# Output tiles, a weight's place in the queue and the casts of a fused attention and soft-MoE kernel

## The chip, the cores and the metric

The kernel runs on one core of a Trainium2 chip. The metric is the device time of one execution in microseconds, as the median of several runs. Smaller is better.

## The reference

Attention with two kinds of masks (four heads see a sliding window of 32 keys, four heads a dilated one), followed by a soft mixture of experts on its output:

```python
scores = scale * np.matmul(q, k.transpose(0, 1, 3, 2))      # B=8, H=8, S=576, D=64
scores = np.where(masks[None, :, :, :], scores, -1000000000.0)
attn = softmax(scores)                                       # over the keys
x = np.matmul(attn, v)  ->  [4608, 512]                      # all tokens, heads side by side

logits = x @ phi                                             # [4608, 32]: 8 experts x 4 slots
slot_input = softmax(logits, axis=0).T @ x                   # [32, 512]
for e in range(E):                                           # E = 8
    h = np.maximum(slot_input[e] @ w1[e], 0.0)               # w1: [8, 512, 1024]
    slot_out[e] = h @ w2[e]                                  # w2: [8, 1024, 512]
out = softmax(logits, axis=1) @ slot_out                     # [4608, 512] float32
```

`softmax` stands for the reference's steps of maximum, exponential and division. The output has 4608 x 512 x 4 bytes, 9.44 MB.

## The kernel before

Attention runs in 32 units (8 batches, 4 pairs of heads each). The raw batch data and, later, the weights live in eight buffers of SBUF, `home0` to `home7`, each 128 partitions by 8192 halves (16 KB a partition). `home{b}` first holds q, k and v of batch `b`. When that batch is done, it takes the weights of expert `e = b`: w1 in the first 4096 columns and w2 in the other 4096. All these loads convert float32 to float16 on their way and are issued by POOL, in the order in which they stand in the program.

`load_w1(e)` (L239) is one transfer of 1 MB written. `load_w2(e)` (L255) depends on the expert, counted from 0:

- experts 0 to 5: one transfer of 1 MB (L262);
- expert 6: by columns; `load_half(6, 0)` (L250) brings the first 256 columns, and the other half is loaded later, in between the pieces of expert 7;
- expert 7: by columns too, and each half of the columns in two pieces (`PIECES`, L271), with the second half of expert 6 ahead of its own second half.

In the loop over units, at `u % 4 == 2`, expert `u // 4` has its w1 loaded (experts 0 to 6) and its w2 (experts 0 to 5). After the loop come w1 of expert 7, then w2 of experts 6 and 7.

From `tail.__enter__()` on (L698) PE, DVE and ACT run in the order that the program has by hand. The experts go in four pairs: `expert_in(pr)` multiplies the slots by w1 of the two experts of a pair (L752) and applies the relu on ACT (L760); `expert_turn(pr)` transposes the result (L766) and copies it to `hTp` on DVE (L771); `expert_out(e, side)` multiplies by w2 and adds up in the PSUM tile `sop` (L781). The pairs are interleaved:

```python
for pr in range(4):
    expert_turn(pr)
    if pr < 2:
        expert_in(pr + 2)
    if pr == 1:
        front_rows(B - 1)
    if pr < 3:
        expert_out(2 * pr)
        expert_out(2 * pr + 1)
```

So the fourth pair's `expert_in`, which needs w1 of experts 6 and 7, stands ahead of `expert_out` of experts 2 to 5.

The last pair's `expert_out` and the output go by `SIDES`: first columns 0 to 255 of `sop`, then 256 to 511. On each side, the sums of experts 6 and 7 are added, the side of `sop` is cast to `so` (its first half on ACT at L840, its second half on DVE at L841), and the first six of twelve output tiles are made for this side. The remaining six tiles follow with all 512 columns at once.

`finish_tile(i, d0, d1)` (L810) makes one output tile: for each of its 2 or 4 blocks of 128 rows, one product on PE (L822) into one of six rotating PSUM tiles, and an eviction with the row's scale, in turn on ACT (L826) and DVE (L828), into the tile `ot`. SP then sends it. Tile 0 of the first side is sent block by block (L832), every other one whole (L834). There are four `ot` tiles in `home0` to `home3`, which the weights of experts 0 to 3 have left by then; tile `i` uses `ots[i % 4]`, so it can be written when tile `i - 4` has been sent. Within an `ot`, the two sides lie in separate halves.

Of the kernel before, what the change touches and what calls it, by code (L numbers as in the profile page):

```python
# [9 lines left out]
FP32 = mybir.dt.float32  # L10
# [15 lines left out]
DMODEL = H * D  # L26
E_EXP = 8
# [33 lines left out]
def kernel(  # L61
# [10 lines left out]
    nc = tc.nc  # L72
# [6 lines left out]
    big = ctx.enter_context(tc.tile_pool(name="big", bufs=1))  # L79
# [5 lines left out]
    for n, (nm, ten, by) in enumerate((("qp", q, nc.sync), ("kp", k, nc.scalar))):  # L85
        first[nm] = stage[0:NP, 768 * n : 768 * n + 768].rearrange("p (g x) -> p g x", g=2)
        by.dma_start(
            out=first[nm],
            in_=ten[0, 0:2].rearrange("h s d -> (h s) d").rearrange("(g p r) d -> p g (r d)", g=2, r=RP),
# [106 lines left out]
    def spread_v(b):  # L196
        nc.vector.tensor_copy(
            out=vd[b % 2][:, :, 0:D], in_=raws[b]["vd"].rearrange("p h r d -> p (h r) d")
        )
# [39 lines left out]
    def load_w1(e):  # L239
        t = homes[e]  # L240
        w1t = t[:, 0:4096].rearrange("p (c f) -> p c f", c=4)
        nc.gpsimd.dma_start(  # L242
            out=w1t.rearrange("p c f -> p (c f)"),
            in_=moe_w1[e].rearrange("(p c) f -> p (c f)", p=128),
        )
        w_tiles[e] = [w1t, t[:, 4096:8192].rearrange("p (c f) -> p c f", c=8)]

    def load_half(e, side):
        d0, d1 = SIDES[side]
        nc.gpsimd.dma_start(  # L250
            out=w_tiles[e][1][:, 0:8, d0:d1],
            in_=moe_w2[e].rearrange("(p c) f -> p c f", p=128)[:, 0:8, d0:d1],
        )

    def load_w2(e):  # L255
        w2t = w_tiles[e][1]
        w2_from = moe_w2[e].rearrange("(p c) f -> p c f", p=128)
        if e == E_EXP - 2:
            load_half(e, 0)
            return  # L260
        if e < E_EXP - 2:
            nc.gpsimd.dma_start(  # L262
                out=w2t.rearrange("p c f -> p (c f)"), in_=w2_from.rearrange("p c f -> p (c f)")
            )
            return
        w2t = w_tiles[e][1] = w2t.rearrange("p c f -> p (c f)").rearrange("p (s c f) -> p s c f", s=2, c=8)
        for n, (d0, d1) in enumerate(SIDES):
            if n == 1:
                load_half(e - 1, 1)
            for c0, c1 in PIECES:  # L270
                nc.gpsimd.dma_start(out=w2t[:, n, c0:c1], in_=w2_from[:, c0:c1, d0:d1])  # L271
# [46 lines left out]
    def scores(u):  # L318
        b, hp = unit(u)
        qT, kT = qTs[u], kTs[u]  # L320
        tiles = []
        for part in range(2):
            st = ps_s.tile([128, 2, 512], FP32, name=f"s{u}_{part}", tag="s")
            if hp < 2:
                todo = [(160 * i, 128 * i, 128 * i, QW) for i in range(3)] if part == 0 else [
                    (0, 384, 384, QW), (QW, 512, 512, 64)]
            else:
                todo = [(DW * cc, CL * (2 * cc + part), CL * (2 * cc + part), CL) for cc in range(2)]
                todo += [(DW * cc + CL, None, CL * (2 * cc + part) + 128, 16) for cc in range(2)]
            for at, k0, q0, n in todo:  # L330
                for g in range(2):
                    ks = q0 - 32 * g - 64 * (at // DW) if k0 is None else k0
                    nc.tensor.matmul(  # L333
                        st[:, g, at : at + n],
                        kT[64 * g : 64 * g + 64, ks : ks + 128],
                        qT[64 * g : 64 * g + 64, q0 : q0 + n],
                        start=True,
                        stop=True,
                    )
            tiles.append(st)  # L340
        return tiles

    def softmax_parts(u, tiles):
        b, hp = unit(u)
        for part in range(2):
            st = tiles[part]
            if hp < 2:
                n = (480, 224)[part]
                pr = raw_pool.tile([128, 2, n], FP16, name=f"pr{u}_{part}", tag=f"pr{part}")
                nc.scalar.activation(out=pr, in_=st[:, :, 0:n], func=AF.Exp, scale=SCALE)  # L350
                for b0, nb, w in ((0, 3, QW),) if part == 0 else ((3, 1, QW), (4, 1, 64)):
                    at = (b0 - 3 * part) * QW
                    nc.vector.tensor_tensor(  # L353
                        out=Pp[:, :, b0 : b0 + nb, 0:w],
                        in0=pr[:, :, at : at + nb * w].rearrange("p h (t c) -> p h t c", c=w),
                        in1=mask[:, None, None, 0:w].broadcast_to([128, 2, nb, w]),
                        op=ALU.mult,
                    )
                continue
            if part == 0:  # L360
                pr = dil_pool.tile([128, 2, 2, 2, DW], FP16, name=f"pd{u}", tag="pd")
            nc.scalar.activation(  # L362
                out=pr[:, part].rearrange("p c e t -> p e c t"),
                in_=st[:, :, 0 : 2 * DW].rearrange("p e (c t) -> p e c t", c=2),
                func=AF.Exp,
                scale=SCALE,
            )
        if hp >= 2:
            dilated_masks(pr)
# [17 lines left out]
    def values(u):  # L387
        for half in range(2):
            normalise(u, half, value_products(u, half))
# [271 lines left out]
    for u in range(NU - 2):  # L661
        st = scores(u + 1)
        values(u)
        softmax_parts(u + 1, st)
        if u + 3 < NU:
            transposes(u + 3)
        b, ph = divmod(u - 4, 4)
        if b >= 0:
            if ph == 1:
                front_logits(b)  # L670
            elif ph == 2:
                front_rows(b)
            elif ph == 3:
                front_slots(b)
        if u == 1:
            spread_phi()
        if u >= 1:
            x_transposes(u - 1)
        if u == NU - 3:
            sixes = batch_sums()  # L680
        if u % 4 == 3 and u // 4 + 1 < B:
            spread_v(u // 4 + 1)
            select_v(u // 4 + 1)
        if u % 4 == 2 and u // 4 < E_EXP - 1:
            load_w1(u // 4)
            if u // 4 < E_EXP - 2:
                load_w2(u // 4)
        if u < 4:
            nc.vector.memset(hTp[u], 0.0)

    load_w1(E_EXP - 1)
    load_w2(E_EXP - 2)
    load_w2(E_EXP - 1)

# [32 lines left out]
        out=siT,  # L727
# [15 lines left out]
    sop = ps_so.tile([128, DMODEL], FP32, name="sop", tag="sop")  # L743
# [50 lines left out]
    for pr in range(4):  # L794
# [7 lines left out]
            expert_out(2 * pr + 1)  # L802

    so = keep.tile([128, DMODEL], FP16, name="so", tag="so")
    ots = [
        big.tile([128, 4, DMODEL], FP32, name=f"ot{i}", tag=f"home{i}") for i in range(4)
    ]
    turn = [0]

    def finish_tile(i, d0, d1):  # L810
        t0, nj = OUT_TILES[i]
        ot = ots[i % 4]
        if d1 - d0 < DMODEL:
            ot = ot.rearrange("p j d -> p (j d)").rearrange("p (s j d) -> p s j d", s=2, j=4)[:, d0 // (d1 - d0)]
        rows_out = out[t0 : t0 + 128 * nj, :].rearrange("(m j) d -> m j d", j=nj)
        for j in range(nj):
            c0, scale = t0 + j, rrow[:, OUT_COLS[i] + j : OUT_COLS[i] + j + 1]
            by_act = turn[0] % 2 == 0
            pool, tag = ((ring, "ring"), (ps_h, "h"), (ps_t, "tp"))[turn[0] % 3]
            fp = pool.tile([128, DMODEL], FP32, name=f"f{turn[0]}", tag=tag)[:, 0 : d1 - d0]  # L820
            turn[0] += 1
            nc.tensor.matmul(  # L822
                fp, ET[:, c0 : c0 + 127 * nj + 1 : nj], so[:, d0:d1], start=True, stop=True
            )
            if by_act:
                nc.scalar.activation(out=ot[:, j], in_=fp, func=AF.Copy, scale=scale)  # L826
            else:
                nc.vector.tensor_scalar(  # L828
                    out=ot[:, j], in0=fp, scalar1=scale, scalar2=None, op0=ALU.mult
                )  # L830
            if i == 0 and d0 == 0:
                nc.sync.dma_start(out=rows_out[:, j, d0:d1], in_=ot[:, j])  # L832
        if i > 0 or d0 > 0:
            nc.sync.dma_start(out=rows_out[:, :, d0:d1], in_=ot[:, 0:nj])  # L834

    for n, (d0, d1) in enumerate(SIDES):
        expert_out(E_EXP - 2, n)
        expert_out(E_EXP - 1, n)
        mid = (d0 + d1) // 2
        nc.scalar.copy(out=so[:, d0:mid], in_=sop[:, d0:mid])  # L840
        nc.vector.tensor_copy(out=so[:, mid:d1], in_=sop[:, mid:d1])  # L841
        for i in range(FIRST_TILES):
            finish_tile(i, d0, d1)
    for i in range(FIRST_TILES, len(OUT_TILES)):
# [35 lines left out]
```

## Time and profile before

| what | us |
|---|---|
| median of three runs | 184.31 (183.91 to 184.97) |
| the profiled execution itself | 184.91 |
| its span, first to last instruction | 183.1 |
| mean granted TensorE clock | 0.945 |

Busy time over the span, from the page: PE 145.5 us (79%), DVE 118.1 (64%), ACT 117.2 (64%), POOL 50.6 (28%). The queue of POOL's transfers takes 96.7% of the 16 DMA engines' span (30.68 MB), and the queue of SP's, which sends the output, 14.1% (9.82 MB). These shares are averages over stages: up to about 130 us attention keeps PE, DVE and ACT busy while the loads stream beside it; after 156 us the output stage has little work on the engines.

How to read it: the chain of waits goes back from the last instruction, at each step to what released it. The view of stretches gives, for each stretch of time, the busy time of PE, PE's weight loads, DVE, ACT and POOL with the number of instructions, and then the granted clock, the share of the DMA engines (it can pass 1, as packets overlap) and the GB/s that they moved, counted as written.

### The profile page before, as it was taken

Reading aid. Unit: us, or ns where it says so; the run is one execution under the profiler, and the core shown is the slowest. Engines: PE = TensorE matmul, PEld = TensorE weight load, DVE = VectorE, ACT = ScalarE, POOL = GpSimd, SP = SyncE. Lnnn points to the kernel's source line nnn. Section 1 sums busy time; section 2 is a strip of 40 time slices with the busy share of each in tenths; the row PEclk is TensorE's granted clock in tenths of the full one; section 3 lists DMA queues with packets and bytes.
Section 4 is the critical chain, followed back from the end, with each engine's and each line's share of the span. In section 5 each row is a group of like instructions: output and inputs, shape, how many; then the busy total and the mean of one; then the engine's idle time right before and its main releaser. Section 6 shows DMA issues by size and latency. Waiting matters only on the chain.

```text
span 183.1 us, 6162 instructions
## 1 busy us (share of the span) xinstructions
PE 145.5 (79%) x2625; PEld 101.2 (55%) x2625; DVE 118.1 (64%) x370; ACT 117.2 (64%) x218; POOL 50.6 (28%) x81
## 2 busy tenths in 40 slices
PE   0797889789889899989979988989799497559300
PEld 0665767576766676767667676667683133334000
DVE  6716896978778778787797877869610002659510
ACT  2076988885987797798799599788213111649410
POOL 7855545555554535300111010034110000000000
PEclk9999999999999999999999999999988958999955
DMA  5999999999999999999999999999999999699996
GB/s 152 192 199 204 200 204 203 201 201 206 198 204 203 200 201 205 224 213 218 217 213 220 211 218 211 224 209 220 211 222 207 195 197 124 233 380 335 430 429 259
DMA packets 31051, 41.18 MB, mean 225 GB/s; under 512 B 1712, under 2 KB 28464, under 8 KB 28720
## 3 DMA queue, kind: packets, MB, share of 16 engines
q0 software_dynamic: 25296, 30.68, 96.7%
q1 hardware_dynamic: 5520, 9.82, 14.1%
q8 instruction: 20, 0.33, 0.6%
q10 hardware_dynamic: 208, 0.29, 0.5%
q14 instruction: 7, 0.06, 0.1%
HBM read 62.02 MB, written 9.44 MB: 390 GB/s over the span
## 4 chain that ended last, share of the span: by engine, by line
DMA 49%; PE 18%; issue 14%; DVE 7%; ACT 6%; POOL 2%; POOLq 0%; ACTq 0%; DVEq 0%
DMA home<-in_moe_w_dram 29%; DMA home<-in_k_dram 9%; DMA out_dram<-ot 6%; DMA home<-in_v_dram 5%; PE sop L781 3%; PE f L822 2%; ACT pd L362 2%; PE sel L208 2%; PE l L470 2%; ACT ot L826 2%; DVE kTd L313 1%; DVE P L373 1%; DVE x L438 1%; PE rgx L452 1%; PE o L417 1%
## 5 line engine op out<-in xcount | busy, mean ns | idle before, releaser
L438 DVE TENSOR_TENSOR x<-o,rc 128x384 f16<-128x384 f32 x64 | 30.1, 483 | 0.6
L350 ACT ACTIVATE pr<-s 128x960 f16<-128x960 f32 (+1 forms) x32 | 24.9, 785 | 0.4 <-PE s L333 0.4
L362 ACT ACTIVATE pd<-s 128x640 f16<-128x640 f32 x32 | 20.9, 706 | 0.7 <-PE s L333 0.7
L167 POOL DMA_DIRECT2D home<-in_v_dram x24 | 16.5, 688 | 16.6 <-DMA home<-in_k_dram 8.7
L828 DVE TENSOR_SCALAR ot<-f,rrow 128x256 f32<-128x256 f32 (+1 forms) x26 | 13.5, 580 | 6.8 <-DMA out_dram<-ot 5.9
L826 ACT ACTIVATE ot<-f,rrow 128x256 f32<-128x256 f32 (+1 forms) x26 | 12.5, 563 | 8.3 <-DMA out_dram<-ot 6.9
L208 PE MATMUL sel<-home,pick 32*128 32x256 f16 x128 | 16.8, 291 | 0.5 <-ACT pr L350 0.5
L452 PE MATMUL rgx<-fixed,x 128*128 128x128 f16 x160 | 14.2, 220 | 3.8 <-ACT qT L313 3.5
L298 ACT COPY qT<-rgq 128x576 f16<-128x576 f16 x16 | 10.3, 641 | 10.4 <-PE rgq L293 10.4
L353 DVE TENSOR_TENSOR Pp<-pr,fixed 128x960 f16<-128x960 f16 (+2 forms) x48 | 16.4, 393 | 0.0
L428 DVE RECIPROCAL rc<-o 128x6 f32<-128x6 f32 x64 | 9.9, 174 | 9.8 <-PE o L417 9.5
L822 PE MATMUL f<-so,ET 128*128 128x256 f16 (+1 forms) x52 | 11.2, 311 | 5.0 <-ACT ot L826 2.9
L242 POOL DMA_DIRECT2D home<-in_moe_w_dram x8 | 4.2, 531 | 36.2 <-PE rgk L308 14.3
L293 PEld LDWEIGHTS <-home 96*64 96x64 f16 x384 | 11.2, 116 | 5.2 <-issue 3.1
L216 ACT CAST vp<-sel 128x512 f16<-128x512 f32 x16 | 9.4, 589 | 7.1 <-PE sel L208 6.8
L452 PEld LDWEIGHTS <-x 128*128 128x128 f16 x160 | 9.6, 97 | 7.2 <-issue 5.1
L458 ACT COPY xT<-rgx 128x512 f16<-128x512 f16 x16 | 9.7, 607 | 4.5 <-PE rgx L452 4.5
L313 DVE COPY kTd<-rgk 128x576 f16<-128x576 f16 x16 | 11.9, 746 | 0.4 <-PE rgk L308 0.4
L417 PE MATMUL o<-vp,Pp 128*128 128x65 f16 x288 | 12.0, 197 | 0.0
L189 POOL DMA_DIRECT2D home<-in_k_dram x15 | 9.8, 650 | 7.7 <-DMA home<-in_q_dram 6.8
L470 PE MATMUL l<-xT,phi 128*128 128x288 f16 x64 | 10.1, 295 | 1.9 <-ACT qT L298 1.7
L313 ACT COPY qT<-rgq 128x576 f16<-128x576 f16 x16 | 10.4, 648 | 1.5 <-PE rgq L308 0.6
(114 smaller groups left out, 290.4 us busy)
## 6 DMA issues: line engine op xcount, KB each, us to landing
home<-in_moe_w_dram POOLq DMA_DIRECT2D x14, 1024.0 KB, 32.8
home<-in_q_dram POOLq DMA_DIRECT2D x15, 288.0 KB, 9.8
home<-in_k_dram POOLq DMA_DIRECT2D x15, 288.0 KB, 10.0
home<-in_v_dram POOLq DMA_DIRECT2D x16, 256.0 KB, 9.8
out_dram<-ot SPq DMA_DIRECT2D x4, 1024.0 KB, 6.7
out_dram<-ot SPq DMA_DIRECT2D x6, 512.0 KB, 3.6
out_dram<-ot SPq DMA_DIRECT2D x7, 256.0 KB, 2.7
home<-in_moe_w_dram POOLq DMA_DIRECT2D x2, 512.0 KB, 26.6
```

What stands on the lines that cost most here:

```text
L167: nc.gpsimd.dma_start(out=dst, in_=v[b, h0 : h0 + n_h, r0 : r0 + 4 * n_p, :].rearrange("h (p r) d -> p h (r d)", r=4),)
L208: nc.tensor.matmul(sel[:, n, 0], pick[rows, r].rearrange("p i j -> p (i j)"), raw[rows, :, r, :], start=(r == 0), stop=(r == 3), tile_posi ...
L313: (nc.scalar.copy if nm == "q" else nc.vector.tensor_copy)(out=dst[:, 0:S].rearrange("c (g p a) -> c g p a", g=4, a=3), in_=rg.rearrange(" ...
L350: nc.scalar.activation(out=pr, in_=st[:, :, 0:n], func=AF.Exp, scale=SCALE)
L353: nc.vector.tensor_tensor(out=Pp[:, :, b0 : b0 + nb, 0:w], in0=pr[:, :, at : at + nb * w].rearrange("p h (t c) -> p h t c", c=w), in1=mask ...
L362: nc.scalar.activation(out=pr[:, part].rearrange("p c e t -> p e c t"), in_=st[:, :, 0 : 2 * DW].rearrange("p e (c t) -> p e c t", c=2), f ...
L417: nc.tensor.matmul(to, lhs, rhs, start=(n == 0), stop=(n == len(mms) - 1), skip_group_check=True)
L438: nc.vector.tensor_tensor(out=x[:, t0 : t0 + nb, D * hl : D * hl + 2 * D].rearrange("p t (h d) -> p t h d", h=2), in0=ot[:, 0:nb, :, 0:D], ...
L452: nc.tensor.transpose(rg[:, 128 * blk : 128 * blk + 128], x[:, blk, hl : hl + 128], ident)
L470: nc.tensor.matmul(lp, phi4[:, kc].rearrange("p a s -> p (a s)"), xT[:, kc, 288 * c : 288 * c + 288], start=(kc == 0), stop=(kc == 3), ski ...
L822: nc.tensor.matmul(fp, ET[:, c0 : c0 + 127 * nj + 1 : nj], so[:, d0:d1], start=True, stop=True)
L826: nc.scalar.activation(out=ot[:, j], in_=fp, func=AF.Copy, scale=scale)
```

## The change

- There are eight `ot` tiles instead of four, two in each of `home0` to `home3`. Tile `i` uses `ots[i % 8]`.
- Tile 0 of the first side is sent whole, in one transfer, as the others are.
- w2 of expert 5 is no longer loaded in the loop but after it, behind w1 of expert 7. That puts w1 of experts 6 and 7 ahead of it in POOL's order.
- `so` is cast by one engine on each side: ACT on the first, DVE on the second.

w2 of experts 6 and 7 is loaded by columns as before.

```diff
         if u % 4 == 2 and u // 4 < E_EXP - 1:
             load_w1(u // 4)
-            if u // 4 < E_EXP - 2:
+            if u // 4 < E_EXP - 3:
                 load_w2(u // 4)
...
     load_w1(E_EXP - 1)
+    load_w2(E_EXP - 3)
     load_w2(E_EXP - 2)
     load_w2(E_EXP - 1)
...
-    ots = [
-        big.tile([128, 4, DMODEL], FP32, name=f"ot{i}", tag=f"home{i}") for i in range(4)
+    pairs = [
+        big.tile([128, 2, 4, DMODEL], FP32, name=f"ot{i}", tag=f"home{i}") for i in range(4)
     ]
+    ots = [pairs[i // 2][:, i % 2] for i in range(8)]
...
-        ot = ots[i % 4]
+        ot = ots[i % 8]
...
-            if i == 0 and d0 == 0:
-                nc.sync.dma_start(out=rows_out[:, j, d0:d1], in_=ot[:, j])
-        if i > 0 or d0 > 0:
-            nc.sync.dma_start(out=rows_out[:, :, d0:d1], in_=ot[:, 0:nj])
+        nc.sync.dma_start(out=rows_out[:, :, d0:d1], in_=ot[:, 0:nj])
...
-        mid = (d0 + d1) // 2
-        nc.scalar.copy(out=so[:, d0:mid], in_=sop[:, d0:mid])
-        nc.vector.tensor_copy(out=so[:, mid:d1], in_=sop[:, mid:d1])
+        (nc.scalar.copy if n == 0 else nc.vector.tensor_copy)(out=so[:, d0:d1], in_=sop[:, d0:d1])
```

## The prediction

> **What bounds the kernel now.** I read the chain of waits first, then the waits, the transfers of the weights, and last the output stage in stretches. The chain of waits, start and length in us:
>
> ```profile
> 121.84 24.28 DMA home<-in_moe_w_dram
> 146.12 0.04 issue
> 146.16 1.89 PE h L752 x14
> ...
> 153.55 0.65 PE sop L781 x16
> 154.20 0.02 issue
> 154.22 0.28 ACT so L840
> 154.50 0.02 issue
> 154.52 0.30 DVE so L841
> ...
> 161.48 2.68 DMA out_dram<-ot
> ```
>
> PE gets its last work from w1 of expert 7 (counted from 0), landing at 146.1. From there PE computes without a pause to the first cast of `so` at 154.22; the casts run one after the other. The rest of the chain alternates with output transfers. The waits from 140 us on say why:
>
> ```profile
> ACT ot L826 <- DMA out_dram<-ot: 6.9, 5, 1.9
> DVE ot L828 <- DMA out_dram<-ot: 5.9, 5, 1.7
> ...
> PE h L752 <- DMA home<-in_moe_w_dram: 2.6, 1, 2.6
> ```
>
> Evictions wait for a buffer whose transfer is still out: 6.9 and 5.9 us. That matters only where the DMA engines then run dry, so I cut the end into stretches (engine busy times, then granted clock, DMA share, GB/s):
>
> ```profile
> 142.40:145.80 3.40, 1.16 (x18) 0.36 (x7) 0.26 (x2) 0.32 (x1) 0.00 (x0) 1.00 1.27 196
> 145.80:152.60 6.80, 6.17 (x62) 2.20 (x61) 0.49 (x3) 0.60 (x1) 0.00 (x0) 0.50 1.44 196
> 154.30:155.50 1.20, 0.64 (x6) 0.58 (x6) 0.51 (x2) 0.52 (x2) 0.00 (x0) 1.00 0.55 75
> 155.50:156.50 1.00, 0.98 (x7) 0.52 (x6) 1.00 (x4) 1.00 (x4) 0.00 (x0) 1.00 0.17 22
> 156.50:158.00 1.50, 0.76 (x4) 0.38 (x4) 0.44 (x2) 0.51 (x2) 0.00 (x0) 1.00 0.58 203
> 160.00:160.50 0.50, 0.00 (x0) 0.00 (x0) 0.33 (x2) 0.14 (x1) 0.00 (x0) 1.00 0.45 162
> 160.50:165.50 5.00, 3.10 (x18) 1.92 (x18) 2.90 (x8) 2.82 (x8) 0.00 (x0) 1.00 1.09 384
> 165.50:166.50 1.00, 1.00 (x7) 0.51 (x5) 1.00 (x4) 1.00 (x3) 0.00 (x0) 1.00 0.38 129
> 169.00:181.40 12.40, 1.76 (x6) 0.39 (x4) 3.69 (x6) 2.95 (x5) 0.00 (x0) 0.67 1.02 427
> ```
>
> Output bytes flow from 156.5 to 181.4. Fed, the stream moves 384 GB/s while half tiles go out and 427 GB/s afterwards. The 9.44 MB are 4.19 MB of half tiles (12 tile halves) and 5.24 MB of whole tiles: 4.19/0.384 + 5.24/0.427 = 10.9 + 12.3 = **23.2 us**. The stage takes 24.9, so it starves for 1.7 us: at 156.5 to 158 (203 of 384 GB/s, 0.7 us lost), 160 to 160.5 (0.3), 165.5 to 166.5 (0.7). The output stage is bandwidth with three holes.
>
> The weights end in a long tail. At 196 GB/s all engines work; 75 GB/s at 154.3 to 155.5 is some 6 of 16, 22 GB/s after that one or two. Those laggards finish at 156.7, which is when the last piece of w2 of expert 7 lands (issued 136.63, 20.1 to landing).
>
> **The weights' order.** All weights go through one queue, landing about every 4.9 us: w1 of 5 at 131.3 (issue 92.15 + 39.1), w2 of 5 at 136.3, w1 of 6 at 141.3, w1 of 7 at 146.1, the first column half of w2 of 6 at 148.8, the two first-side pieces of w2 of 7 at 150.75 and 151.5, then 154.1, 156.1 and 156.7. Putting w2 of 5 behind w1 of 7 moves w1 of 6 to 136.3 and w1 of 7 to 141.2, and w2 of 5 to 146.1. One issue of 0.53 us on POOL moves from 96.84 to 122.4 and pushes the three issues behind it by 0.53. That costs nothing as long as the queue is full: at 121.84 it still holds w2 of 4, w1 of 5 and w1 of 6, some 15 us. Without that cover it would cost the 0.53. The last three issues on POOL wait for the landing of the transfer eight places earlier (127.31 after 127.1, 131.81 after 131.3, 136.63 after 136.3); the places are the same after the change, and a landing sits at each of those times, so they stay. SP has nothing queued then.
>
> **PE up to the first cast.** PE reaches the fourth pair's w1 products at 143.15 and no longer waits there. By rows at full clock: 16 products 1.09 (the row at 140.92), row sums 0.45, `sop` of experts 2 and 3 1.04, transposes 0.41, `hTp` 0.26, `sop` of 4 and 5 1.04, to 147.4; expert 5's half starts at 146.9, 0.8 after its w2 has landed. Transposes and `hTp` again: 148.1. Now PE waits for w2 of 6 (148.8) and of 7 (151.5); two products and their drain, 0.25: cast at 151.75 instead of 154.22. The next term is late instead: the weights of the first side.
>
> PE then idles about 2.4 us between 148.8 and 151.5. In the stretch 142.4 to 145.8 PE was busy 1.16 of 3.40 us, and the next 6.8 ran at clock 0.50. The same would slow the first products here: 16 `sop` products took 1.04 at full and 1.77 to 1.90 at half clock, so two `sop` and two `f` products cost 0.1 to 0.2 more. The Trainium skill (TensorE: Matmul & The Clock Gate, Part 1: The HAM clock gate) says that PE falls to half rate after about one idle window of 3.4 us; the two stretches above agree with that. By it the idle time would merely have moved, as I assume.
>
> **Casts.** 0.59 now (154.22 to 154.81, serial). One engine casting 128x256 is nearest to an eviction of that shape: 0.47 on ACT, 0.48 on DVE. Saves 0.12 per side. DVE's cast of side two waits at the head of DVE's queue, but everything behind it needs `so` anyway.
>
> **First tile in one transfer.** It goes after its second eviction, 0.88 after the cast as now (154.81 to 155.69): 152.22 + 0.88 = 153.1, with one SP issue fewer (0.4). A 128 KB issue had bytes flowing 0.9 us later; the 256 KB ones behind it took 1.2. So bytes flow at about **154.3** instead of 156.5, and the hole of 156.5 to 158 closes: the next 256 KB need 0.68 us on the wire, and SP issues one each 0.58.
>
> **Eight tiles.** Tiles 4 and 5 get their own buffers on both sides, whole tiles 6 and 7 too, and 8 to 11 reuse tiles long sent. The holes at 160 and 165.5 close. Should SP's transfers also wait for the landing of the one eight places earlier, as POOL's do, seven would still be queued, 1.8 MB or more. Without waits the evictions run at 0.2 us per block (two engines, 0.40 each) against 0.34 on the wire, and 0.36 against 0.61 for whole rows.
>
> **The sum.** Starting at 154.3, outputs now run beside the weights' tail. Each transfer spreads over the engines, so it ends with the slowest, and the laggards owe weights until 156.7 whatever goes between. Their end is 156.7 + 23.2 = 179.9 if they never run dry, against 181.4: minus 1.5. The holes alone add up to 1.7; I take 1.6. So the 2.2 us of earlier start buy nothing by themselves; only the closed holes do.
>
> Do they run dry? At 154.3 a laggard owes 2.4 us of weights and 10.9/2 = 5.45 us of side-one output: busy until 162.1. Side two needs the last weights, then 0.25 + 0.47 + 0.88 + 1.2 = 2.8 us until its bytes flow. How long the outputs hold these weights up is not in the trace of before. Bounds: not at all (156.7), or behind all of side one (162.1). I take equal shares, since on one engine a 1 KB output row (384 GB/s over 16) and a 512 B weight row (196 over 16) both take some 42 ns: 154.3 + 4.8 = 159.1, bytes at 161.9. Just in time. The Trainium skill (DMA: Bandwidth & Descriptors, Queues, rings and completion order) says each engine goes round robin between its queues, packet by packet; no run here shows it. By that the sum would be the same 179.9.
>
> The profiled execution took 184.91 with a span of 183.1; minus 1.6 gives 183.3 and a span of 181.5. It lies 0.6 above the median of 184.31, so against the median: **182.7**.
>
> **Rivals.**
> - *The early start pays* (0.17). If the laggards lag for a reason that outputs relieve, only total bytes count: 154.3 + 23.2 + 0.6 (0.11 MB of weights left at 196 GB/s) = 178.1, plus a hole before side two of 0 to 1.5. Gain 1.8 to 3.3: 181.0 to 182.5. For it: 10 of 16 engines idle at 154.3. Against: a transfer has landed only with its slowest part.
> - *Weights behind output* (0.18, slower). Side two's weights land at 162.1, its bytes flow at 164.9, then 5.45 + 12.3: 182.6 instead of 181.4, **185.5**. It decides once those weights land later than 160.9. For it: side one offers 2.1 MB at once, and no wait holds it back now. Against: the weights are queued long before.
> - *Half of it, or not what it says* (0.20). Weights at about 160, or the halves of a `home` still treated as one buffer, so that the holes of 0.3 and 0.7 stay: gain 0.3 to 1.0, 183.3 to 184.0. If only the new weight order failed, output would start at 156.3 and end at 179.7 all the same, seen in the trace and not in the time.
> - *My forecast* (0.45): 182.2 to 183.3.
>
> **Chances.** About 0.5% (183.39 to 185.23) can be told from no change. Faster: 0.43 of the forecast, 0.17, 0.02 of the halfway case: 0.62. Same: 0.02 + 0.17 + 0.02 of the slower one: 0.21. Slower: 0.16 + 0.01 = 0.17. The range, 181.0 to 185.2, leaves out the far half of the slower case and a little of the early one.
>
> **What would show it.** The chain should lose its wait before L752 and show PE waiting for w2 at L781; the first `so` cast at 151.5 to 152, the first output issue near 153.1; no waits of L826 and L828 for `out_dram`; side two's cast at 159 to 160; DMA at 384 and 427 GB/s without holes. Output bytes ending later than 181.4, or a side-two cast after 161.5, would make me wrong.

## The result and the profile after

| | before | after |
|---|---|---|
| median of 6 runs, us | 184.43 (183.91 to 184.97) | 182.93 (182.75 to 182.97) |
| ratio, 95% interval | | 0.9917 (0.9899 to 0.9935) |
| span of the profiled execution, us | 183.1 | 181.2 |

The time fell by 1.5 us; 182.7 had been forecast. Some executions of either kernel fall into a slower state (188.9 us against a median of 184.6 for the kernel before in the first experiments), and the ratios here and below leave such runs out. The chain of waits of the changed kernel (start, length in us) no longer passes through the products with w1 or through output transfers:

```profile
136.72 20.10 DMA home<-in_moe_w_dram
156.82 0.04 issue
156.86 0.30 PE sop L782 x2
...
157.25 0.43 DVE so L838
...
158.17 2.48 DVE ot L830 x7
160.64 0.28 issue
160.92 6.40 DVE ot L830 x10
```

It now hangs on the last piece of w2 of expert 7 (issued at 136.72, landed at 156.82), then on side two's cast and on evictions that no transfer holds up. The chain as shown ends with the last evictions, at 168.0; for the output stream that runs on behind them the stretches below stand. The waits from 140 us on agree: no eviction waits for `out_dram` any more, and PE waits for w2 instead of w1.

```profile
PE sop L782 <- DMA home<-in_moe_w_dram: 3.4, 4, 1.6
...
ACT ot L828 <- PE f L824: 2.1, 1, 2.1
```

The same end in stretches (engine busy times, granted clock, DMA share, GB/s):

```profile
146.20:152.40 6.20, 2.56 (x37) 1.26 (x38) 0.30 (x3) 0.37 (x1) 0.00 (x0) 1.00 1.45 196
154.30:155.50 1.20, 1.20 (x7) 0.63 (x5) 1.20 (x4) 1.20 (x3) 0.00 (x0) 0.50 1.04 270
155.50:156.50 1.00, 0.96 (x15) 0.41 (x15) 0.70 (x2) 0.48 (x2) 0.00 (x0) 0.75 1.14 356
156.50:158.00 1.50, 0.67 (x10) 0.34 (x5) 0.42 (x1) 0.00 (x0) 0.00 (x0) 1.00 1.09 383
158.00:165.00 7.00, 6.25 (x31) 3.19 (x29) 6.83 (x14) 6.84 (x15) 0.00 (x0) 1.00 1.09 384
166.00:177.50 11.50, 0.97 (x3) 0.19 (x2) 1.98 (x4) 1.31 (x2) 0.00 (x0) 0.66 1.01 423
177.50:179.70 2.20, 0.00 (x0) 0.00 (x0) 0.00 (x0) 0.00 (x0) 0.00 (x0) 0.50 0.33 132
```

The three holes are gone: 383 and 384 GB/s without a break while half tiles go out, then 423. New is the last line. Before, the output ended sharply at 181.4; now most engines are done at 177.6, and a few carry on at 132 GB/s in the mean until 179.5. Output began some 2 us earlier (154.5) and its bulk ended 3.8 us earlier, but the end moved by less than 2.

### The profile page after: what moved, and what is told of

The parts are those of the page before. It is cut to its first block, busy times and chain, and to the rows that moved or that the text cites. A ratio compares the mean times of both kernels' runs of the same rounds, so it can differ in the third digit from the quotient of the medians.

```text
span 181.2 us, 6142 instructions
## 1 busy us (share of the span) xinstructions
PE 144.1 (80%) x2625; PEld 101.4 (56%) x2625; DVE 117.8 (65%) x369; ACT 117.1 (65%) x217; POOL 50.7 (28%) x81
## 4 chain that ended last, share of the span: by engine, by line
PE 28%; DMA 26%; DVE 16%; ACT 13%; issue 7%; POOL 2%; DVEq 0%; ACTq 0%; POOLq 0%
DMA home<-in_moe_w_dram 11%; DMA home<-in_k_dram 9%; ACT pd L362 8%; PE sel L208 6%; DMA home<-in_v_dram 5%; DVE ot L830 5%; PE l L470 4%; PE rgx L452 3%; DVE P L373 3%; PE rgq L293 3%; PE o L417 3%; DVE kTd L313 3%; DVE x L438 3%; ACT qT L298 2%; ACT qT L313 2%
## 5 line engine op out<-in xcount | busy, mean ns | idle before, releaser
L438 DVE TENSOR_TENSOR x<-o,rc 128x384 f16<-128x384 f32 x64 | 30.1, 484 | 0.6
```

The source lines that it names most:

```text
L438: nc.vector.tensor_tensor(out=x[:, t0 : t0 + nb, D * hl : D * hl + 2 * D].rearrange("p t (h d) -> p t h d", h=2), in0=ot[:, 0:nb, :, 0:D], ...
```

## Experiment 1: the change without the new weight order

```diff
-            if u // 4 < E_EXP - 3:
+            if u // 4 < E_EXP - 2:
                 load_w2(u // 4)
...
-    load_w2(E_EXP - 3)
```

> The whole change except the weights' order (w2 of expert 5 stays in the loop, ahead of w1 of 6 and 7). Theory (the last DMA engines to finish the weights set the end: they owe weights until 156.8 and then 23 us of output, so an earlier start on the others buys nothing): first output issue back near 155.7, output bytes still end at 179.5 to 180, time 1.4 to 1.7 us under the kernel before, the same as the full change. Rival (the early start pays): the first output comes 2.3 us later than with the full change, so the end does too, about 0.5 us slower than the kernel before to 0.3 faster.

Measured: ratio 0.9919 (0.9892 to 0.9946) to the kernel before, the same as with the order. The time does not miss it. The profile is no test of the start: in this execution PE did not fall to half clock before the first cast, which came at 151.17 with the first output issue at 152.59, so the old order did not delay the start here. Its last weights landed at 156.1, 0.7 us before those of the changed kernel, and its bytes end about as much earlier, with a tail too:

```profile
155.50:164.00 8.50, 6.88 (x38) 3.48 (x38) 7.00 (x15) 6.58 (x15) 0.00 (x0) 1.00 1.09 383
165.00:177.30 12.30, 1.22 (x5) 0.19 (x2) 2.23 (x4) 1.55 (x3) 0.00 (x0) 0.66 1.01 421
177.30:179.00 1.70, 0.00 (x0) 0.00 (x0) 0.00 (x0) 0.00 (x0) 0.00 (x0) 0.50 0.31 128
```

## Experiment 2: eight tiles alone

```diff
-    ots = [
-        big.tile([128, 4, DMODEL], FP32, name=f"ot{i}", tag=f"home{i}") for i in range(4)
+    pairs = [
+        big.tile([128, 2, 4, DMODEL], FP32, name=f"ot{i}", tag=f"home{i}") for i in range(4)
     ]
+    ots = [pairs[i // 2][:, i % 2] for i in range(8)]
...
-        ot = ots[i % 4]
+        ot = ots[i % 8]
```

> The kernel before with eight output tiles for four and nothing else. Theory: the holes at 160 to 160.5 and 165.5 to 166.5 close (1.0 us), the one at 156.5 to 158 (0.7) stays in part, since tile 0 still goes in two short transfers: 1.0 to 1.4 us under the kernel before. Rival (each part brings its share, the order most of it): less than 0.5 us.

Measured: 0.9918 (0.9882 to 0.9954), 1.5 us. That is the gain of the whole change. The stretches, with tile 0 still sent in two pieces and the casts shared:

```profile
155.00:157.00 2.00, 2.00 (x24) 1.06 (x24) 2.00 (x6) 2.00 (x6) 0.00 (x0) 1.00 0.71 206
157.00:166.00 9.00, 7.31 (x37) 3.65 (x34) 8.48 (x18) 8.11 (x18) 0.00 (x0) 1.00 1.09 383
167.00:179.30 12.30, 0.12 (x1) 0.00 (x0) 0.95 (x2) 0.32 (x1) 0.00 (x0) 0.68 1.00 421
```

From 157 on nothing is lost. What was left of the first hole fell in the time in which the last engines still had weights to move.

## Experiment 3: the weight order alone

```diff
-            if u // 4 < E_EXP - 2:
+            if u // 4 < E_EXP - 3:
                 load_w2(u // 4)
...
+    load_w2(E_EXP - 3)
```

> The kernel before with only the weights' order changed. Theory: the first cast comes at 151.9 instead of 154.2, but with four tiles the evictions of tile 4 still wait for tile 0's landing, which the slow engines hold until about 157; two or three holes stay, and the time falls by 0 to 0.8 us. Rival (the early start pays): 1.5 us or more.

Measured: 1.0001 (0.9969 to 1.0033), nothing. The waits of the evictions are those of the kernel before (us in total, times, longest):

```profile
ACT ot L827 <- DMA out_dram<-ot: 6.1, 5, 1.9
DVE ot L829 <- DMA out_dram<-ot: 5.1, 5, 1.7
```

In the profiled execution PE came to the first w1 products 5.8 us later than in the changed kernel (142.80 against 137.04), so the first cast came at 154.57 and this trace does not show the early start at work. That the order alone buys no time rests on the times alone.

## Experiment 4: everything but the eight tiles

```diff
-    pairs = [
-        big.tile([128, 2, 4, DMODEL], FP32, name=f"ot{i}", tag=f"home{i}") for i in range(4)
+    ots = [
+        big.tile([128, 4, DMODEL], FP32, name=f"ot{i}", tag=f"home{i}") for i in range(4)
     ]
-    ots = [pairs[i // 2][:, i % 2] for i in range(8)]
...
-        ot = ots[i % 8]
+        ot = ots[i % 4]
```

> The whole change except the eight tiles (four again). Theory: waits of both evictions for out_dram come back, some 10 us in all, holes of together 0.5 to 1.2 us in the output stream after 157; time 0.3 to 1.0 us under the kernel before, so 0.5 to 1.2 above the full change. Rival (the tiles don't matter once output starts early): within 0.3 us of the full change.

Measured: 1.0024 (0.9997 to 1.0051). The expected 0.3 to 1.0 us under the kernel before did not come; the holes were larger than expected. Here the first cast did come early (152.34) and the output stream started and stopped again:

```profile
154.30:158.00 3.70, 1.60 (x8) 0.96 (x7) 0.85 (x2) 0.64 (x3) 0.00 (x0) 0.50 1.00 293
158.00:160.20 2.20, 1.56 (x18) 0.56 (x17) 1.67 (x5) 1.56 (x4) 0.00 (x0) 0.50 0.14 50
...
165.00:167.20 2.20, 2.20 (x7) 0.88 (x6) 1.77 (x5) 2.03 (x5) 0.00 (x0) 0.50 0.74 263
```

The waits behind it:

```profile
ACT ot L827 <- DMA out_dram<-ot: 7.7, 4, 3.1
DVE ot L829 <- DMA out_dram<-ot: 6.5, 4, 2.9
```

At 158 to 160.2 the DMA engines do nearly nothing (50 GB/s): four tiles are out, tile 4 waits for tile 0's landing, and side two's cast, behind those evictions on DVE, comes at 160.19 instead of 157.25. The early start is spent in this hole. Shown so far: the eight tiles are the whole gain, and the other parts add nothing that these runs can tell.

## Experiments 5 and 6: a later start

If the start sets the end, a delay passes through. If the engines that finish the weights last set it, a delay up to their finish is free.

```diff
         (nc.scalar.copy if n == 0 else nc.vector.tensor_copy)(out=so[:, d0:d1], in_=sop[:, d0:d1])
+        if n == 0:
+            warm(5, ring, "ring")
```

> The changed kernel with 20 idle products of 128 columns on PE between the first cast of so and the first output product: 1.1 us at full clock, 2.1 at half, added to the start of the output. Theory (the slowest DMA engines set the end): output bytes start at 155.5 to 156.5 instead of 154.4, still before 156.8, and end at 179.6 as before; time within 0.4 us of the changed kernel's (ratio to the kernel before about 0.992). Rival (the start sets the end): 1.1 to 2.1 us slower than the changed kernel, ratio about 1.000.

Measured: 0.9938 (0.9910 to 0.9967) against 0.9917, so about 0.4 us of the delay arrived, which the intervals cannot tell from nothing. PE spent 2.9 us on the idle products, and the first output issue moved by 2.25 us (155.57 for 153.32):

```profile
155.50:156.50 1.00, 1.00 (x7) 0.69 (x6) 1.00 (x3) 1.00 (x4) 0.00 (x0) 0.50 0.15 19
...
157.00:167.00 10.00, 8.45 (x54) 4.28 (x53) 9.51 (x20) 8.89 (x19) 0.00 (x0) 0.98 1.09 384
168.00:179.90 11.90, 0.28 (x1) 0.00 (x0) 1.12 (x2) 0.49 (x1) 0.00 (x0) 0.63 1.01 425
179.90:181.90 2.00, 0.00 (x0) 0.00 (x0) 0.00 (x0) 0.00 (x0) 0.00 (x0) 0.50 0.09 35
```

Output begins at 156.8, just after the last weights have landed (156.5 here), and the tail has gone: all engines stop at about 180.0, 0.5 us after the changed kernel. The 2.25 us came out of the time in which most engines had been ahead of the few.

The same with `warm(15, ring, "ring")`:

> The same with 60 idle products, 3.3 us at full clock and 6.4 at half. Theory: only what passes 156.8 costs, the delay less about 2.4: 1 to 4 us slower than the changed kernel. Rival: the whole delay, 3.3 to 6.4 us slower.

Measured: 1.0276 (1.0234 to 1.0319), 6.6 us above the changed kernel's ratio, from two runs 1.5 us apart (188.64 and 190.15). The idle products took 8.4 us rather than 6.4, and the first issue moved to 160.76. Against the changed kernel that is 7.4 us of delay; less 2.4 the theory gives 5.0, the rival 7.4, and the time lies between them, so by itself it decides for neither. The bulk of the bytes, which flow from 162.0, ends at 185.4, some 23 us later as in the other runs. Between the two delays the issue moved by 5.2 us and the time by 6.2, so past the weights all of it passes through, but the 1.0 us more is not explained. Part of it shows in the trace: although the weights were long done (1 GB/s in the first stretch), the output ends with a tail here too, 26 GB/s from 185.6 on, which is about one engine's sixteenth of the 425 GB/s before it.

```profile
155.50:161.50 6.00, 6.00 (x46) 5.00 (x45) 1.31 (x4) 1.53 (x5) 0.00 (x0) 0.58 0.01 1
...
185.00:185.60 0.60, 0.00 (x0) 0.00 (x0) 0.00 (x0) 0.00 (x0) 0.00 (x0) 0.50 0.46 184
185.60:186.40 0.80, 0.00 (x0) 0.00 (x0) 0.00 (x0) 0.00 (x0) 0.00 (x0) 0.50 0.06 26
```

## Experiment 7: no weights behind the first output

```diff
-            for c0, c1 in PIECES:
+            for c0, c1 in PIECES if n == 0 else ():
...
-        w2t = w_tiles[e][1][:, side] if e == E_EXP - 1 else w_tiles[e][1][:, :, d0:d1]
+        w2t = w_tiles[e][1][:, 0] if e == E_EXP - 1 else w_tiles[e][1][:, :, d0:d1]
```

> The changed kernel without the load of the second column half of expert 7's w2 (the products of the second side use the first half's weights again): 0.5 MB of 16 less at the end of the weights' queue. Theory: the slow engines owe weights only until 154.1, when the other half of expert 6 lands, so output is no longer held by them; it starts at 154.4 as now and ends at 154.4 + 23.2 = 177.6, sharply and without a tail: 1.9 to 2.1 us under the changed kernel. Rival (the tail of 177.7 to 179.6 belongs to the output transfers themselves): output still ends above 179, at most 0.5 us gained.

This kernel leaves out half of the last w2, so it serves to read the time alone. Measured: 0.9829 (0.9808 to 0.9850), 1.6 us under the changed kernel's ratio where 1.9 to 2.1 were expected; the span is 179.3 for 181.2. The first output issue is at 152.99, 0.3 us from the changed kernel's, yet the end moves and the tail is gone:

```profile
154.00:155.00 1.00, 1.00 (x6) 0.46 (x4) 1.00 (x4) 1.00 (x4) 0.00 (x0) 0.50 0.77 272
...
177.00:177.60 0.60, 0.00 (x0) 0.00 (x0) 0.00 (x0) 0.00 (x0) 0.00 (x0) 0.50 0.82 335
177.60:179.30 1.70, 0.00 (x0) 0.00 (x0) 0.00 (x0) 0.00 (x0) 0.00 (x0) 0.50 0.01 2
```

So the changed kernel's tail belongs to the weights, not to the output. The landing of the first output transfer says the same. In the changed kernel (issue at 153.32):

```profile
DMA to landing us min/median/max: 4.3/4.3/4.3
```

and here, without weights behind it (issue at 152.99):

```profile
DMA to landing us min/median/max: 2.5/2.5/2.5
```

The difference of 1.8 us is what the last part of this transfer waited while there were weights still to move.

## Experiment 8: four tiles by sides

```diff
-FIRST_TILES = 6
+FIRST_TILES = 4
```

> The changed kernel with four tiles by sides for six (FIRST_TILES = 4), so that 2.1 MB go at the 384 GB/s of half rows and 7.34 MB at the 427 of whole rows: 5.5 + 17.2 = 22.7 us of stream for 23.2. Theory: the slow engines have 2.7 us of side one after 156.8, until 159.5, and side two's bytes come at 159.9: 0.5 saved and 0.4 lost, 0 to 0.4 us under the changed kernel. Rival (the start sets the end): the fast engines run dry at 157.1 and wait 2.8 us, 1 to 2 us slower than the changed kernel.

Measured: 0.9985 (0.9958 to 1.0012), 1.3 us slower than the changed kernel. The expectation failed.

```profile
157.40:160.30 2.90, 2.51 (x10) 1.49 (x11) 2.10 (x5) 1.92 (x5) 0.00 (x0) 0.50 0.17 61
160.30:162.50 2.20, 2.20 (x7) 0.80 (x6) 1.72 (x3) 1.87 (x3) 0.00 (x0) 0.50 1.09 382
```

Four tiles of side one last the fast engines until 157.4, and side two's bytes come at 160.3, so even the slow engines, which by the theory had output until 159.5, ran dry for 0.8 us. From 160.3 there are 1.05 MB at 384 GB/s and 7.34 at 427 to go, 19.9 us, hence 180.2; the bytes end at 180.4. The rival's 1 to 2 us came true in number, and by its mechanism too: engines ran dry between the sides. I had taken side two at 159.9 and left out that nothing then stands against a late side two. With six tiles, side one lasts 154.5 + 5.45 = 160.0, just to side two's bytes (issue 158.7 + 1.2 = 159.9).

## Experiments 9 to 11: w2 of expert 6 in one transfer

The changed kernel, run again beside these two:

> The changed kernel once more, as the measure for the two variants beside it: ratio to the kernel before 0.990 to 0.9935.

Measured: 0.9909 (0.9874 to 0.9943).

```diff
-        if e == E_EXP - 2:
-            load_half(e, 0)
-            return
-        if e < E_EXP - 2:
+        if e < E_EXP - 1:
...
-            if n == 1:
-                load_half(e - 1, 1)
```

> The changed kernel with w2 of expert 6 loaded whole, in one transfer, instead of by column halves: 1 MB in some 4.9 us instead of 5.3. Theory (the slow engines' weights set the end): the last weights land at 156.3 to 156.5 instead of 156.8 and the end moves by as much, 0.2 to 0.5 us under the changed kernel, although the first cast comes some 2 us later (153.8 for 151.9) and output bytes start at 156.5. Rival (the start sets the end): 2 us slower than the changed kernel.

Measured: 0.9972 (0.9944 to 1.0001), 1.2 us slower than the changed kernel beside it. Neither end of the expectation held.

```profile
154.30:155.50 1.20, 1.20 (x7) 0.88 (x6) 0.77 (x2) 0.98 (x3) 0.00 (x0) 0.50 0.31 41
155.50:156.50 1.00, 1.00 (x7) 0.69 (x5) 1.00 (x4) 1.00 (x3) 0.00 (x0) 0.50 0.00 0
```

The weights did end earlier: at 155.5 to 156.5 nothing moves at all. But the output bytes start only at 156.5 (first issue at 155.31, PE at half clock), so now the start is the later of the two and sets the end, at about 180.0. That is 0.5 us after the changed kernel's; the other 0.7 us of the measured 1.2 does not show in this trace, whose own time (183.41) lies 0.3 us under this variant's median.

The same with `FIRST_TILES = 5`:

> whole6 with five tiles by sides for six: 3.15 MB at 384 GB/s and 6.29 at 427, 22.9 us of stream for 23.2. Side one lasts 4.1 us from 156.5, to 160.6, and side two's bytes come at 159.2 to 159.6, so nothing runs dry. Theory: 0.3 us under whole6, 0.5 to 0.8 under the changed kernel. Rival (side two comes later than side one lasts, as with four tiles): 0.3 us or more above whole6.

Measured: 0.9958 (0.9931 to 0.9985), not to be told from whole6, and above the changed kernel. Its first issue came at 155.94, 0.6 later than in whole6, so its start was later still. The expected gain did not come in either. No complete variant beat the changed kernel.

## Why the prediction was right, point by point

**The end is the later of two, plus some 23 us.** In us, with the start of the bytes as the first issue plus 1.2:

| kernel | bytes start | last weights land | bytes end | end less the later |
|---|---|---|---|---|
| changed | 154.5 | 156.8 | 179.5 | 22.7 |
| without the new order (experiment 1) | 153.8 | 156.1 | 178.8 | 22.7 |
| eight tiles alone (experiment 2) | 155.4 | 156.5 | 179.5 | 23.0 |
| short delay (experiment 5) | 156.8 | 156.5 | 180.1 | 23.3 |
| without the last w2 half (experiment 7) | 154.2 | 153.9 | 177.6 | 23.4 |
| w2 of expert 6 whole (experiment 10) | 156.5 | 155.9 | 180.0 | 23.5 |
| before | 156.5 | 156.7 | 181.4 | 24.7, with the three holes |

The ends are read from stretches of 0.2 us and leave out the last packets of one or two engines, which run 0.2 to 0.5 us longer in each of these.

The forecast was 156.7 + 23.2 = 179.9 for the changed kernel; 179.5 was measured. The step that the earlier start buys nothing by itself held: experiment 5 shows it by delaying the start. The times of experiments 1 and 3, with the order taken away and brought alone, agree, but in neither trace did the order move the first cast as forecast.

The trace does not name the engines, but the view of the transfer queues bears out that those with late weights are those of the tail. With all 16 engines at work the weights' queue takes 145% of their time and the output's 102 to 109%, so that a queue's share gives an estimate of how many engines serve it. In the changed kernel, in three stretches of half a microsecond from 155.0 on, the weights' queue takes 37.3%, 25.8% and 14.5%: 4.1, 2.8 and 1.6 engines. In the same three stretches 23.0 us later, from 178.0 on, the output's queue takes 30.1%, 22.0% and 12.0%: 4.7, 3.5 and 1.9 engines.

**The closed holes.** 1.6 us was forecast, 1.5 measured, and experiment 2 shows that the eight tiles alone bring it. The casts were priced too high: one of 128x256 took 0.37 us on ACT and 0.42 on DVE, not the 0.47 and 0.48 of an eviction of that shape, so that 0.2 us a side were saved on the 0.59 and not 0.12. It does not show in the time, nor does the single transfer, since on the first side both only move the start.

**PE's path.** The first cast was forecast at 151.75 and came at 151.90; the first issue at 153.1 came at 153.32. PE fell to half clock after the wait for w2, as assumed (0.50 from 152.6 to 156.0). The cast ended at 152.27, 0.05 late; the other 0.17 us by which the issue was late lie in the products and evictions behind it, most of them at half clock, which had been priced at 0.1 to 0.2.

**The step that failed: equal shares.** The weights beside the output were to be slowed to 159.1, with the cast of side two at 159 to 160. They were not slowed at all: the last piece took 20.10 us to landing, as before (20.1), and side two's cast came at 157.25. Nor did the weights go slower beside the output on the way there. These are the queues' shares of the 16 engines' time, with weights alone in the kernel before and with output beside them in the changed one:

| from, us | before, weights | changed, weights | changed, output |
|---|---|---|---|
| 154.5 | 57.9% | 44.8% | 62.2% |
| 155.0 | 46.0% | 37.3% | 81.3% |
| 155.5 | 21.3% | 25.8% | 87.5% |
| 156.0 | 12.6% | 14.5% | 99.7% |

By the estimate above the output has 12.0, 12.9 and 14.7 engines in the last three rows, about as many as the weights leave. In other traces the last piece took 19.7 to 20.1 us to landing with output beside it for 1.6 us or more (experiments 1, 4 and 8), 20.6 with 0.9 us of it (experiment 2), and 20.3 and 20.5 with none (experiments 3 and 5). The output was what waited, as the landings in experiment 7 show too. The lower bound held, "not at all", and so the rival in which the weights fall behind the output had no place. The Trainium skill (DMA: Bandwidth & Descriptors, Queues, rings and completion order) says that an engine goes round robin between its queues; by that the last piece should have landed later than without output beside it, and it did not. For these 2.4 us the measurement decides against it. The sum was spared, since the slow engines owe the same 23 us in either order.

**The rival of the early start** got one thing right: at 154.5 most engines were free, and their bulk of output ended 3.8 us earlier. The time goes by the few that were not.

What stays open: why these few engines finish the weights up to 4 us after the others (the trace does not name engines), the tail of experiment 6, and 0.7 us of the loss in experiment 10.

## What to carry to other kernels

When one stream of transfers follows another, look at how sharply the first one ends: if its rate tapers off, its last engines set when the second one ends, and starting the second before they are through gained nothing here. What counts then is that the second is never without work, so give it buffers before giving it an earlier start; with too few buffers an early start turns into a hole. A stage cut in parts also needs a first part long enough to last until the second one's bytes flow.

## What the runs showed of the hardware

Output transfers beside the tail of converting loads did not slow those loads (20.1 us to landing with and without them), and the first of them took 4.3 us to land instead of 2.5. PE's clock halved after stretches that were a third work: the one with 1.16 us of work in 3.40 was followed by 6.8 us at 0.50, and in the changed kernel 1.02 us of work between 149.2 and 152.6 were followed by 3.4 at 0.50. So they agree with the prediction's idle window only if so much work counts as idle; the 3.4 us before, with 1.90 us of work, were followed by full clock. PE's arrival at the first w1 products varied from 137.0 to 142.8 between profiled executions; with the eight tiles alone it came 4.1 us later than in the changed kernel (141.09 for 137.04), and the output ended at about the same 179.5.
